# Moving two layer norms and three transposes one step later, splitting the last output block, and sharing the copies of one row between two engines

## The chip, the cores and the metric

The kernel runs on one core of a Trainium2 chip. The metric is the device time of one execution in microseconds (us). Every kernel was executed several times; the numbers below are medians with the range. Runs in the fast state (granted TensorE clock 0.998 to 0.999 of full speed) may be compared with each other.

## The reference, cut to what matters

A sequence of 2048 rows of 640 features goes through two pairs of layers. Layer A is a Fourier filter, layer B an attention over segments of 32 tokens with 32 heads. Both are applied to the layer norm of the row and added to it.

```python
def _layernorm(x, axis=-1, eps=1e-05):
    m = jnp.mean(x, axis=axis, keepdims=True)
    v = jnp.var(x, axis=axis, keepdims=True)
    return (x - m) / jnp.sqrt(v + eps)
...
    x = A_x
    x = x + _A_ref(_layernorm(x, axis=-1), A_w_r, A_w_i)
    x = x + _B_ref(_layernorm(x, axis=-1), B_mem0, B_Wq, B_Wk, B_Wv, B_Wo, B_seg_len)
    x = x + _A_ref(_layernorm(x, axis=-1), A_w_r, A_w_i)
    x = x + _B_ref(_layernorm(x, axis=-1), B_mem0, B_Wq, B_Wk, B_Wv, B_Wo, B_seg_len)
    return x
```

In the kernel the 2048 rows lie as 16 tiles of 128 partitions; a "row" below is such a tile of 128x640.

## The kernel before

Three places matter. The first is the *token stage*, which ends layer A: the inverse transform (tiles `psg`, `psy` in PSUM), the residual add, the statistics and the layer norm of each row, and the transposes of the normed rows that layer B starts from (`pstr`). It runs twice, at 73 and at 835 us. Its loop fixes the order of work on each engine by hand:

```python
LEAD, LAG, EARLY, LAST = 0, 7, 10, 10
ADDED, SQUARED = (0, 1, 2, 3, 4, 6), (1, 3, 6) + (15,)   # rows added by VectorE; rows with statistics by ScalarE
...                                                      # (cut: definitions of the steps)
for i in range(16 + 1):
    ...
    last = i >= LAST
    early = i < EARLY
    ...
    if not early and i % 2 == 1:
        norm((i - 5) // 2)           # norm q: rows 2q and 2q+1, VectorE, needs the inverse deviation of q
    if not last:
        ready(False)                 # statistics on VectorE of the row added a step ago
    if i < 16:
        spectrum_d(i)                # PE: psg i, ScalarE copies it out
    ready(True)                      # statistics on ScalarE, with two small operations of GpSimd
    ...
    for s0 in range(16):
        if turn(s0) == i:
            tokens(s0)               # PE: psy; VectorE or ScalarE adds it to the row
    if early and i >= 5 and i % 2 == 1:
        norm((i - 5) // 2)
    ...
    if i >= 4 and i % 2 == 0:
        inverse((i - 4) // 2, nc.gpsimd)   # six small GpSimd operations, 2.2 us in the trace (80.38 to 82.55)
    ...
    if i >= 8 and i % 4 < 3:         # transposes of a group of four rows, in three parts of 2, 2 and 1 chunks
        n = i % 4
        by_dve_jobs = n != 1 and i < 16
        jobs = handoff.rows_out(handoff.rows_in(pp, xna, i // 4 - 2, 2 * n), by_dve_jobs)
        ...
```

So norm 0 stands in step 5, norm 1 in step 7, norm 2 in step 9, and the first three transposes in steps 8, 9, 10. The tiles `psg` and `psy` share three buffers; the transposes have two.

The second place, called the *seam* below, is the end of the first attention layer, with the first transform of the next layer A row by row (`stage1_tile`), and the verdict of a check inside the kernel, which is read from PSUM (`pc`):

```python
def stage1_tile(self, pp, tag, xn_row, s0):
    nc = self.tc.nc
    for c0, c1 in ((0, 3), (3, 5)):
        ps = pp.tile([128, 512], FP32, name="ps1", tag=tag)
        for ch in range(c0, c1):
            nc.tensor.matmul(ps[:, (ch - c0) * 128:(ch - c0 + 1) * 128], lhsT=xn_row[:, ch * 128:(ch + 1) * 128], rhs=self.T[:, s0, :], start=True, stop=True)
        nc.scalar.copy(out=self.YT[:, c0:c1, :, s0, :], in_=ps[:, 0:(c1 - c0) * 128].rearrange("p (c g k) -> p c g k", c=c1 - c0, k=8))
...
def result(self, flag_col, ranges=False):          # the check's verdict
    nc = self.tc.nc
    vmax = self.tmp("vmax", 1, 1)
    nc.vector.tensor_reduce(out=vmax[:], in_=self.pe[:, 0:self.NC], axis=AX.X, op=ALU.max)      # reads PSUM (pc)
    ...
    nc.vector.tensor_single_scalar(out=ok[:], in_=self.pe[:, self.NC:self.NC + 2], scalar=127.5, op=ALU.is_ge)   # and again
```

After them the spectrum stage opens a new PSUM pool and its first matmuls write the tile `ab`.

The third place is the end of the kernel, the output projection of the last rows:

```python
def run(self, x, lhs_of, psx, first, n_first, pa, xns, check, acc, flag_col):
    ...
    for t in range(16):
        lhs = lhs_of(t)
        for k in (2 * t, 2 * t + 1):
            ps = first[k] if k < len(first) else psx()
            ...
            self.accumulate(ps, k, lhs, n_first if k < len(first) else 0, H)    # 32 matmuls of 320 columns
            c0 = k % 2 * 320
            nc.vector.tensor_tensor(out=x[:, t, c0:c0 + 320], in0=ps[:, 0:320], in1=x[:, t, c0:c0 + 320], op=ALU.add)
        if nxt is None:
            nc.sync.dma_start(out=self.xd[:, t, :], in_=x[:, t, :])
        ...
```

Of the kernel before, what the change touches and what calls it, by code (L numbers as in the profile page):

```python
# [13 lines left out]
ALU = mybir.AluOpType  # L14
# [184 lines left out]
class LayerA:  # L199
# [211 lines left out]
# [3 lines that stand above are left out]
            ps = pp.tile([128, 512], FP32, name="ps1", tag=tag)  # L414
            for ch in range(c0, c1):
                nc.tensor.matmul(ps[:, (ch - c0) * 128:(ch - c0 + 1) * 128], lhsT=xn_row[:, ch * 128:(ch + 1) * 128], rhs=self.T[:, s0, :], start=True, stop=True)
            nc.scalar.copy(out=self.YT[:, c0:c1, :, s0, :], in_=ps[:, 0:(c1 - c0) * 128].rearrange("p (c g k) -> p c g k", c=c1 - c0, k=8))

    def spectrum(self, late_loads=(), handoff=None):
        tc, g, YT, Fd, K = self.tc, self.g, self.YT, self.Fd, self.K  # L420
# [171 lines left out]
    def tokens(self, x_dst, xn_dst, handoff=None):  # L592
        tc, g, UT, Gd, Ti, x = self.tc, self.g, self.UT, self.Gd, self.Ti, self.x
        nc = tc.nc
# [13 lines left out]
            nc.scalar.copy(out=Gs[s0 % 3], in_=psg[:, :, 0:NF])  # L608

        LEAD, LAG, EARLY, LAST = 0, 7, 10, 10  # L610
        ADDED, SQUARED = (0, 1, 2, 3, 4, 6), (1, 3, 6) + (15,)
        nm = wk.tile([128, 16], FP32, name="lnnm", tag="lnnm")

        def tokens(s0):
# [58 lines left out]
        def norm(q):  # L673
            xno = xna[:, 2 * q:2 * q + 2, :]
            for t in range(2):
                _ln_scale(nc, mv[q][:, t:t + 1, :], rs[q][:, t:t + 1], x[:, 2 * q + t:2 * q + t + 1, :], xno[:, t:t + 1, :], 1)
                flush()
            nc.sync.dma_start(out=xnd[:, 2 * q:2 * q + 2, :], in_=xno)

        with tc.manual_schedule(engines={nc.tensor.engine, nc.scalar.engine, nc.vector.engine}):  # L680
            moved, late, by_dve_jobs = [], [], False
            turn = lambda s0: s0 + (2 if LEAD <= s0 < LAG else 1)
            for i in range(16 + 1):
                held = moved if by_dve_jobs else []
                for f in moved if not held else moved[:1]:
                    f()
                held, moved = held[1:], []
                if late:
                    late.pop(0)()
                last = i >= LAST  # L690
                early = i < EARLY
                done = [s0 for s0 in range(16) if turn(s0) == i - 1]
                ready = lambda act: [stats(s0) for s0 in done if (s0 in SQUARED) == act and s0 < 15]
                if last:
                    ready(False)
                if not early and i % 2 == 1:
                    norm((i - 5) // 2)
                if not last:
                    ready(False)
                if i < 16:  # L700
                    spectrum_d(i)
                ready(True)
                for f in held:
                    f()
                    flush()
                for s0 in range(16):
                    if turn(s0) == i:
                        tokens(s0)
                if early and i >= 5 and i % 2 == 1:
                    norm((i - 5) // 2)  # L710
                for f in late:
                    f()
                late = []
                if i >= 4 and i % 2 == 0:
                    inverse((i - 4) // 2, nc.gpsimd)
                if handoff is None:
                    continue
                if i < 10:
                    handoff.wv_piece(i)
                if i == 5:  # L720
                    handoff.memory(pp)
                if i == 16:
                    for s0 in range(10):
                        handoff.add_u(pp, xna[:, s0, :], s0)
                if i >= 8 and i % 4 < 3:
                    n = i % 4
                    by_dve_jobs = n != 1 and i < 16
                    jobs = handoff.rows_out(handoff.rows_in(pp, xna, i // 4 - 2, 2 * n), by_dve_jobs)
                    if n == 1:
                        late = jobs  # L730
                    else:
                        moved = jobs
            flush()
            act_stats(15)
            norm(6)
            inverse(7, nc.vector)
            if handoff is not None:
                for s0 in range(10, 14):
                    handoff.add_u(pp, xna[:, s0, :], s0)
                handoff.do(moved)  # L740
                second = handoff.rows_in(pp, xna, 2, 2)
            norm(7)
            if handoff is not None:
                for s0 in (14, 15):
                    handoff.add_u(pp, xna[:, s0, :], s0)
                handoff.finish(pp)
                handoff.do(handoff.rows_out(second, False))
                pairs = [handoff.rows_in(pp, xna, 3, 2 * n, ps=handoff.big(pp)) for n in range(2)]
                ones = [handoff.rows_in(pp, xna, 2, 4)]
                vb = [handoff.guess1(pp, 0)]  # L750
                ones.append(handoff.rows_in(pp, xna, 3, 4))
                handoff.do(handoff.rows_out(pairs[0], True))
                handoff.do(handoff.rows_out(pairs[1], False))
                vb.append(handoff.guess1(pp, 1))
                handoff.do(handoff.rows_out(ones[0], True))
                handoff.guess1_out(0, vb[0], nc.scalar.copy)
                vb.append(handoff.guess1(pp, 2))
                handoff.guess1_out(1, vb[1], nc.scalar.copy)
                handoff.do(handoff.rows_out(ones[1], True))
                vb.append(handoff.guess1(pp, 3))  # L760
                handoff.guess1_out(2, vb[2], nc.scalar.copy)
                vb.append(handoff.guess1(pp, 4))
                handoff.guess1_out(3, vb[3], nc.vector.tensor_copy)
                handoff.guess1_out(4, vb[4], nc.scalar.copy)
# [773 lines left out]
class _FastOut:  # L1538
# [2 lines left out]
        self.tc, self.g, self.nxt = tc, g, nxt  # L1541
        self.xd = r16(env["x_dst"]) if env["x_dst"] is not None else None

    def accumulate(self, ps, k, lhs, h0, h1):
        c0 = k % 2 * 320
        for h in range(h0, h1):
            self.tc.nc.tensor.matmul(ps[:, 0:320], lhsT=lhs(h, k // 2), rhs=self.g["Wo_sb"][:, h, c0:c0 + 320], start=(h == 0), stop=(h == H - 1))  # L1547

    def run(self, x, lhs_of, psx, first, n_first, pa, xns, check, acc, flag_col):
        nc, nxt = self.tc.nc, self.nxt  # L1550
        early = {t: c for c, t in enumerate((3, 5) if nxt is not None else (3, 5, 7, 9, 11))}
# [3 lines that stand above are left out]
                ps = first[k] if k < len(first) else psx()  # L1555
                if nxt is None and k == 31:
                    self.tc.mark_branch_hint_location("general")
                self.accumulate(ps, k, lhs, n_first if k < len(first) else 0, H)
                c0 = k % 2 * 320
                nc.vector.tensor_tensor(out=x[:, t, c0:c0 + 320], in0=ps[:, 0:320], in1=x[:, t, c0:c0 + 320], op=ALU.add)  # L1560
            if nxt is None:
                nc.sync.dma_start(out=self.xd[:, t, :], in_=x[:, t, :])
            else:
                if t:
                    nxt.stage1_tile(pa, "pss", xns[(t - 1) % 3], t - 1)
                st, mv = _ln_tiles(nc, self.g["ln"])
                _ln_stats(nc, st, mv, x[:, t, :], 0)
                _ln_apply(nc, self.g["ln"], mv, x[:, t:t + 1, :], xns[t % 3].unsqueeze(1), 1, self.g, on_dve=True)
            if t == 2:
                check.prepare(acc)  # L1570
            if t == 4:
                check.begin(acc)
            if t == 6 and nxt is not None:
                nxt.tables(gate=xns[5 % 3][0:1, 0:1])
            if t in early:
                check.block(early[t])
            if t - 1 in early:
                check.vote(early[t - 1])
            if nxt is None and t == 12:
                check.result(flag_col, True)  # L1580
        if nxt is not None:
            for c in range(len(early), 5):
                check.block(c)
            nxt.stage1_tile(pa, "pss", xns[15 % 3], 15)
            for c in range(len(early), 5):
                check.vote(c)
            check.result(flag_col, True)
# [290 lines left out]
```

## Time and profile before

| | us |
|---|---|
| time, median of 3 runs (range) | 1554.5 (1554.37 to 1554.54) |
| profiled span | 1552.9 |
| first token stage, first `psg` to PE's restart on `psu` | 73.22 to 106.72 |
| last `ps` of the first transform to first `ab` | 786.54 to 787.71 |
| end of the last add to the end of the span | 1545.67 to 1552.9 |

The prediction shows the lines of the page and the timelines on which its reading rests. One thing that it does not show is the middle of the token stage in the chain of waits. That view walks back from the last instruction; its columns are start, length, and who did what, with the line of the program. Kernel before:

```profile
80.38 0.24 POOL lnrs L124
80.70 0.74 POOL lnnb L125
...
86.04 0.20 POOL lnrs L129
86.27 0.45 DVE A1tok_S L134
...
91.29 0.20 POOL lnrs L129
91.52 0.80 DVE A1tok_S L134 x2
```

From 80.4 to 86.3, and again up to 91.5, the chain goes through GpSimd (POOL): two inverse deviations in a row, and each time VectorE (DVE) stands at a norm (L134) until GpSimd's last small operation (L129) is through. An inverse took GpSimd 2.2 us (80.38 to 82.55), or 2.7 us with two operations that go with a ScalarE square among its six (88.76 to 91.49); L125 took 0.71 to 0.73 us of that, the others about 0.2. GpSimd is busy for 16% of the span only, and yet it holds the stage here: VectorE started none of its later work while it stood at these norms (1.08 us before the one at 86.27, 0.42 before the one at 91.52).

### The profile page before, as it was taken

Reading aid. Unit: us, or ns where it says so; the run is one execution under the profiler, and the core shown is the slowest. Engines: PE = TensorE matmul, PEld = TensorE weight load, DVE = VectorE, ACT = ScalarE, POOL = GpSimd, SP = SyncE. Lnnn points to the kernel's source line nnn. Section 1 sums busy time; section 2 is a strip of 40 time slices with the busy share of each in tenths; the row PEclk is TensorE's granted clock in tenths of the full one; section 3 lists DMA queues with packets and bytes.
Section 4 is the critical chain, followed back from the end, with each engine's and each line's share of the span. In section 5 each row is a group of like instructions: output and inputs, shape, how many; then the busy total and the mean of one; then the engine's idle time right before and its main releaser. Section 6 shows DMA issues by size and latency. Waiting matters only on the chain.

```text
span 1552.9 us, 36725 instructions
## 1 busy us (share of the span) xinstructions
PE 1535.5 (99%) x14554; PEld 1081.3 (70%) x14555; DVE 816.6 (53%) x2418; ACT 764.9 (49%) x2229; POOL 246.0 (16%) x337
## 2 busy tenths in 40 slices
PE   9999999999999999999999999999999999999997
PEld 7776666666666666777777776666666666667775
DVE  7873555555556545632368545654556545553111
ACT  5574655556555565511126655556555565562000
POOL 2530111112111121100035201112111121110000
PEclk9999999999999999999999999999999999999999
DMA  4780343344533444645114523443434434337241
GB/s 173 230 299 27 111 170 122 137 140 135 178 123 136 136 136 149 201 117 162 51 54 159 178 83 125 136 150 121 172 124 140 148 125 166 124 107 228 79 127 53
DMA packets 168839, 214.90 MB, mean 138 GB/s; under 512 B 8144, under 2 KB 134360, under 8 KB 168656
## 3 DMA queue, kind: packets, MB, share of 16 engines
q1 hardware_dynamic: 168080, 210.15, 40.9%
q8 instruction: 116, 1.90, 0.5%
q0 software_dynamic: 576, 2.30, 0.4%
q14 instruction: 67, 0.55, 0.1%
HBM read 167.32 MB, written 45.10 MB: 137 GB/s over the span
## 4 chain that ended last, share of the span: by engine, by line
PE 92%; DVE 4%; POOL 1%; ACT 1%; issue 1%; DMA 0%; ACTq 0%; DVEq 0%; POOLq 0%
PE psv L1267 19%; PE psk L1201 19%; PE psx L1547 18%; PE psq L1201 18%; PE pso L1351 4%; PE pss L1277 4%; PE ab L449 2%; PE psl L1304 1%; PE psq L1225 1%; PE X L480 1%; PE psu L541 1%; DVE lnst L650 1%; PE psm L977 1%; PE psg L1708 1%; PE psvb L1640 1%
## 5 line engine op out<-in xcount | busy, mean ns | idle before, releaser
L1201 PEld LDWEIGHTS <-bB_S 128*128 128x128 bf16 x3180 | 261.5, 97 | 181.3 <-issue 1.1
L1260 DVE CAST bB_S<-psk 128x495 bf16<-128x495 f32 (+3 forms) x320 | 191.6, 599 | 281.3 <-PE psk L1201 276.9
L1547 PE MATMUL psx<-Wo_sb,bB_S 128*128 128x320 bf16 x2048 | 288.7, 299 | 0.1
L1280 ACT ACTIVATE bB_S<-pss 128x269 bf16<-128x269 f32 (+5 forms) x576 | 208.7, 387 | 138.3 <-PE pss L1277 137.9
L1547 PEld LDWEIGHTS <-bB_S 128*128 128x128 bf16 x2048 | 196.8, 98 | 73.9 <-DVE bB_S L1365 0.7
L1320 POOL TENSOR_TENSOR bB_S<-bB_S,bB_S 128x535 f32<-128x535 f32 x90 | 111.7, 1254 | 795.2 <-DVE bB_S L1312 762.2
L1245 ACT ACTIVATE bB_S<-psq 128x96 bf16<-128x96 f32 x300 | 152.1, 507 | 172.6 <-PE psq L1201 172.6
L1365 DVE TENSOR_TENSOR bB_S<-pso,bB_S 128x480 bf16<-128x480 f32 (+1 forms) x320 | 193.0, 603 | 55.8 <-PE pso L1351 47.2
L1281 DVE TENSOR_TENSOR bB_S<-bB_S,maskf 128x269 bf16<-128x269 bf16 (+5 forms) x576 | 159.5, 290 | 114.3 <-ACT bB_S L1280 114.3
L1269 ACT CAST bB_S<-psv 128x512 bf16<-128x512 f32 (+1 forms) x288 | 162.4, 564 | 81.0 <-PE psv L1267 81.0
L1267 PE MATMUL psv<-bB_S,B1hT_S 128*128 128x256 bf16 x1360 | 168.8, 272 | 0.0
L1267 PE MATMUL psv<-bB_S,B2hT_S 128*128 128x256 bf16 x1360 | 168.8, 272 | 0.0
L1201 PE MATMUL psk<-B1hT_S,bB_S 128*128 128x495 bf16 (+3 forms) x800 | 164.2, 343 | 0.0
L1201 PE MATMUL psk<-B2hT_S,bB_S 128*128 128x495 bf16 (+3 forms) x800 | 164.2, 343 | 0.0
L1201 PE MATMUL psq<-B1hT_S,bB_S 128*128 128x495 bf16 (+5 forms) x780 | 156.0, 336 | 0.5 <-DVE bB_S L1646 0.5
L1201 PE MATMUL psq<-B2hT_S,bB_S 128*128 128x495 bf16 (+5 forms) x780 | 156.0, 336 | 0.5 <-DVE bB_S L1646 0.5
L1267 PEld LDWEIGHTS <-B1hT_S 128*128 128x128 bf16 x1360 | 129.8, 98 | 24.3
L1267 PEld LDWEIGHTS <-B2hT_S 128*128 128x128 bf16 x1360 | 129.8, 98 | 24.3
L1277 PE MATMUL pss<-bB_S 128*128 128x132 bf16 (+8 forms) x1152 | 137.5, 219 | 0.0
L1277 PEld LDWEIGHTS <-bB_S 128*128 128x128 bf16 x1152 | 95.4, 97 | 55.1
L1351 PE MATMUL pso<-bB_S,bB_S 128*128 128x132 bf16 (+8 forms) x1152 | 118.6, 219 | 0.2
L1351 PEld LDWEIGHTS <-bB_S 128*128 128x128 bf16 x1152 | 89.7, 98 | 32.3 <-DVE oTmf L1366 1.9
(299 smaller groups left out, 1438.5 us busy)
## 6 DMA issues: line engine op xcount, KB each, us to landing
bB_S<-Rd SPq DMA_DIRECT2D x124, 535.0 KB
oTx_d<-bB_S SPq DMA_DIRECT2D x60, 512.0 KB
bB_S<-oTx_d SPq DMA_DIRECT2D x46, 512.0 KB
bB_S<-in_B_Wq_dram SPq DMA_DIRECT2D x32, 320.0 KB
bB_S<-in_B_Wk_dram SPq DMA_DIRECT2D x32, 320.0 KB
bB_S<-in_B_Wv_dram SPq DMA_DIRECT2D x32, 320.0 KB
Wo_sb<-in_B_Wo_dram SPq DMA_DIRECT2D x4, 1280.0 KB
B1wv_S<-in_B_Wv_dram SPq DMA_DIRECT2D x10, 512.0 KB
```

Of the source, the lines that this page charges most:

```text
L1201: nc.tensor.matmul(ps, lhsT=w[:, ch, hh * 128:(hh + 1) * 128], rhs=src[:, ch, lo:hi], start=(ch == 0), stop=(ch == 4))
L1245: nc.scalar.mul(out=qv[:, :, 0:SEG], in_=x_view(ps, o, n)[:, :, 1:SW], mul=scale)
L1260: nc.vector.tensor_copy(out=KTs[h % 2][:, lo:hi], in_=ps[:, 0:hi - lo])
L1267: nc.tensor.matmul(ps[:, i * 256:(i + 1) * 256], lhsT=hT[:, ch, st.hcol((t + i) * 128):st.hcol((t + i) * 128) + 128], rhs=w["Wv"][:, ch, : ...
L1269: nc.scalar.copy(out=V[:, t:t + n, :].rearrange("p a b -> p (a b)"), in_=ps[:, 0:n * 256])
L1277: nc.tensor.matmul(ps[:, off - o0:off - o0 + hi - lo], lhsT=KT[:, t * 128:(t + 1) * 128], rhs=QT[:, lo:hi], start=True, stop=True)
L1280: nc.scalar.activation(out=E[:, 0:n], in_=ps[:, 0:n], func=ACTF.Exp)
L1281: nc.vector.tensor_tensor(out=P[:, o0:o0 + n], in0=E[:, 0:n], in1=bs.mask[:, o0:o0 + n], op=ALU.mult)
L1320: nc.gpsimd.tensor_tensor(out=acc, in0=acc, in1=part, op=ALU.add)
L1351: nc.tensor.matmul(pso[:, lo - q0:hi - q0], lhsT=V[:, t, (h % 2) * 128:(h % 2 + 1) * 128], rhs=P[:, off:off + hi - lo], start=(i == 0), st ...
L1365: nc.vector.tensor_tensor(out=oT.rearrange("p (r s j) -> p r s j", r=16, j=2)[:, :, s0:s0 + ns, :], in0=byclass(po), in1=rx, op=ALU.mult)
L1547: self.tc.nc.tensor.matmul(ps[:, 0:320], lhsT=lhs(h, k // 2), rhs=self.g["Wo_sb"][:, h, c0:c0 + 320], start=(h == 0), stop=(h == H - 1))
```

## The change

Its intent is to let the engines find their inputs ready. In the token stage, norms 0 and 1 stand a step later, behind that step's residual add, the first three transposes a step later as well; row 5 is added by VectorE instead of by two identity matmuls and a ScalarE copy, and row 4's statistics go from VectorE to ScalarE. At the seam, VectorE empties the second half of the first transform's last row. At the end, the last 320 columns come in two pieces of 192 and 128, each with its own add and store. The diff, with unchanged context cut:

```diff
@@ stage1_tile
-            nc.scalar.copy(out=self.YT[:, c0:c1, :, s0, :], in_=ps[:, 0:(c1 - c0) * 128].rearrange(...))
+            (nc.vector.tensor_copy if s0 == 15 and c0 else nc.scalar.copy)(out=self.YT[:, c0:c1, :, s0, :], in_=ps[:, 0:(c1 - c0) * 128].rearrange(...))
@@ tokens
-        ADDED, SQUARED = (0, 1, 2, 3, 4, 6), (1, 3, 6) + (15,)
+        ADDED, SQUARED = tuple(range(7)), (1, 3, 4, 6) + (15,)
...
+                due = {6: 0, 8: 1}.get(i, (i - 5) // 2 if i >= 9 and i % 2 else None)
...
-                if not early and i % 2 == 1:
-                    norm((i - 5) // 2)
+                if not early and due is not None:
+                    norm(due)
...
-                if early and i >= 5 and i % 2 == 1:
-                    norm((i - 5) // 2)
+                if early and due is not None:
+                    norm(due)
...
-                if i >= 8 and i % 4 < 3:
-                    n = i % 4
+                if 9 <= i < 12 or i >= 12 and i % 4 < 3:
+                    n = i % 4 - (i < 12)
@@ class _FastOut
-    def accumulate(self, ps, k, lhs, h0, h1):
+    def accumulate(self, ps, k, lhs, h0, h1, lo=0, hi=320):
...
-            self.tc.nc.tensor.matmul(ps[:, 0:320], ..., rhs=self.g["Wo_sb"][:, h, c0:c0 + 320], ...)
+            self.tc.nc.tensor.matmul(ps[:, 0:hi - lo], ..., rhs=self.g["Wo_sb"][:, h, c0 + lo:c0 + hi], ...)
...
                 if nxt is None and k == 31:
                     self.tc.mark_branch_hint_location("general")
+                    for lo, hi in ((0, 192), (192, 320)):
+                        ps = ps if lo == 0 else psx()
+                        self.accumulate(ps, k, lhs, 0, H, lo, hi)
+                        nc.vector.tensor_tensor(out=x[:, t, 320 + lo:320 + hi], in0=ps[:, 0:hi - lo], in1=x[:, t, 320 + lo:320 + hi], op=ALU.add)
+                        nc.sync.dma_start(out=self.xd[:, t, 0 if lo == 0 else 320 + lo:320 + hi], in_=x[:, t, 0 if lo == 0 else 320 + lo:320 + hi])
+                    continue
...
             if nxt is None:
-                nc.sync.dma_start(out=self.xd[:, t, :], in_=x[:, t, :])
+                if t < 15:
+                    nc.sync.dma_start(out=self.xd[:, t, :], in_=x[:, t, :])
```

More of the change, by code (lines that the diff above doesn't have):

```diff
@@ L416, in stage1_tile @@
                 nc.tensor.matmul(ps[:, (ch - c0) * 128:(ch - c0 + 1) * 128], lhsT=xn_row[:, ch * 128:(ch + 1) * 128], rhs=self.T[:, s0, :], start=True, stop=True)
-            nc.scalar.copy(out=self.YT[:, c0:c1, :, s0, :], in_=ps[:, 0:(c1 - c0) * 128].rearrange("p (c g k) -> p c g k", c=c1 - c0, k=8))
+            (nc.vector.tensor_copy if s0 == 15 and c0 else nc.scalar.copy)(out=self.YT[:, c0:c1, :, s0, :], in_=ps[:, 0:(c1 - c0) * 128].rearrange("p (c g k) -> p c g k", c=c1 - c0, k=8))
     def spectrum(self, late_loads=(), handoff=None):
@@ L1542, in __init__ @@
         self.xd = r16(env["x_dst"]) if env["x_dst"] is not None else None
-    def accumulate(self, ps, k, lhs, h0, h1):
+    def accumulate(self, ps, k, lhs, h0, h1, lo=0, hi=320):
         c0 = k % 2 * 320
         for h in range(h0, h1):
-            self.tc.nc.tensor.matmul(ps[:, 0:320], lhsT=lhs(h, k // 2), rhs=self.g["Wo_sb"][:, h, c0:c0 + 320], start=(h == 0), stop=(h == H - 1))
+            self.tc.nc.tensor.matmul(ps[:, 0:hi - lo], lhsT=lhs(h, k // 2), rhs=self.g["Wo_sb"][:, h, c0 + lo:c0 + hi], start=(h == 0), stop=(h == H - 1))
     def run(self, x, lhs_of, psx, first, n_first, pa, xns, check, acc, flag_col):
```

## The prediction

> **What bounds the kernel now.** I read the page first, then the chain that ended last, then the timelines of three stretches that the diff touches.
>
> ```profile
> PE 1535.5 (99%) x14554; PEld 1081.3 (70%) x14555; DVE 816.6 (53%) x2418; ACT 764.9 (49%) x2229; POOL 246.0 (16%) x337
> ```
> ```profile
> PE 92%; DVE 4%; POOL 1%; ACT 1%; issue 1%; DMA 0%; ACTq 0%; DVEq 0%; POOLq 0%
> ```
>
> TensorE (PE) owns 92% of the chain; all else is 8% of 1553 us. The diff leaves the long attention stages alone, so it can only win fractions of a microsecond at a few seams: the two token stages (73 to 107 us, and 835 to 869 us, row for row the same), the seam at 787 us between the first attention layer and the second transform, and the end. First the token stage, VectorE (DVE) alone, then all engines, then the chain:
>
> ```profile
> 82.58 0.80 DVE L134 TENSOR_SCALAR A1tok_S<-A1x_S,lnmv,lnrs 128x640 bf16<-128x640 bf16 x2 [0.69 <-POOL lnrs L129]
> 83.45 0.82 DVE L630 TENSOR_TENSOR A1x_S<-psy,A1x_S 128x640 bf16<-128x640 f32 x1
> 86.27 0.45 DVE L134 TENSOR_SCALAR A1tok_S<-A1x_S,lnmv,lnrs 128x640 bf16<-128x640 bf16 x1 [1.08 <-POOL lnrs L129]
> 91.52 0.80 DVE L134 TENSOR_SCALAR A1tok_S<-A1x_S,lnmv,lnrs 128x640 bf16<-128x640 bf16 x2 [0.42 <-POOL lnrs L129]
> ```
> ```profile
> 84.32 0.99 PE L607 MATMUL psg<-A1gt_S,A1UT_S 128*128 128x321 bf16 x6 [0.35 <-DVE A1x_S L630]
> ...
> 87.20 0.45 PE L1661 MATMUL pstr<-ident,A1tok_S 128*128 128x128 bf16 x5 [0.20 <-DVE A1tok_S L134]
> ...
> 88.72 0.43 PE L622 MATMUL psy<-A1x_S,ident 128*128 128x320 bf16 x2 [0.24 <-DVE A1x_S L633]
> ```
> ```profile
> 102.48 0.13 DVE lnmv L658
> 102.61 0.08 issue
> 102.69 0.31 POOL lnrs L124
> ...
> 106.22 0.46 DVE A1tok_S L134
> 106.67 0.05 issue
> 106.72 0.32 PE psu L1618 x5
> ```
>
> DVE, in program order, stands at norms 0, 1 and 2 (L134) until GpSimd (POOL) has the inverse deviation; behind it wait the PSUM buffers and transposes that PE needs. From 86.27 the chain runs through DVE with hardly a gap up to the last inverse (102.69) and PE's restart at 106.72. So the stage ends when DVE does, with PE hardly less loaded. Now the seam and the end:
>
> ```profile
> 786.95 0.72 ACT A2YT_S L417 x2
> 787.67 0.04 issue
> 787.71 2.92 PE ab L449 x20
> ```
> ```profile
> 1545.18 0.49 DVE L1560 TENSOR_TENSOR bB2x_S<-psx,bB2x_S 128x320 bf16<-128x320 f32 x1 [3.85 <-PE psx L1547]
> 1545.70 0.33 SPq L1562 DMA_DIRECT2D out_dram<-bB2x_S  x1
> ```
> ```profile
> L1834 SPq EVENT_SEMAPHORE  x9: 17/17/17, 1548.9 to 1551.2; - x9
> ...
> L1834 SPq COMPARE_BRANCH  x1: 50/50/50, 1546.1 to 1546.1; - x1
> ```
>
> At 787 us PE waits for two ScalarE (ACT) copies in a row. At the end SyncE issues the last store, branches at 1546.1, executes its first wait past the branch only at 1548.9 and its last at 1551.2.
>
> [...]the POOL L124 took 0.43 us beginning at 91.57, inside DVE's L134, and 0.23 us at 80.38, outside one. I allow 0.2 us for that below.[...] Here 16 transposes of 128 columns took 0.89 us in the chain, 56 ns each[...]. [...] The DMA view agrees that all its packets are over by 1547.5.[...]
>
> **Part 1, the token stage.** Four edits: norms 0 and 1 go one step later, behind that step's residual add; the first three transpose groups go from steps 8, 9, 10 to 9, 10, 11; row 5's residual is added by DVE, so two identity matmuls leave PE (2 x 0.137 = 0.27 us) and a 0.69 us copy leaves ACT; row 4's statistics go from DVE (0.89 + 0.20 busy) to an ACT square (0.83 + 0.19). The order comparison shows just this, and that DVE is in step again at row 11's statistics (97.16 before).
>
> I lay DVE's new order end to end with issue intervals of the old trace (L134 pair 0.71, add 0.85, add with accumulator 0.73, statistics 0.79, transposed copy 0.57 to 0.63), starting at aggregate 2 at 81.68. Add 4 begins at 82.37, as soon as PE has psy 4; norm 0 at 83.1 (its inverse is ready at 82.55); add 5 83.8; statistics 5 84.7; add 6 85.5; norm 1 at 86.4. So norm 1's wait (1.08) all but goes and add 4 comes 1.08 earlier, add 6 2.4 earlier. PE's waits go with them: psg 8 no longer waits (0.5 us of gap at 83.8 to 84.3 by issue intervals), the transposes no longer wait for norm 1 (0.5), psy 8 no longer for add 6 (0.4). What is new: statistics 7 ends near 88.0, but POOL begins inverse 2 only after add 6 (86.3) and needs about 2.7 us (88.76 to 91.49 before), so norm 2 waits until 89.1 to 89.4, a new 1.2 us. The first transpose copies now stand behind norm 2, so the third transpose group, needing the buffer of the first, waits some 0.6 us at 91.8. Continuing: copies 89.9 and 91.3, statistics 9 92.3, norm 3 93.1, statistics 10 94.4, statistics 11 at 96.0 to 96.2 against 97.16. PE comes to step 13 at 94.7 to 94.9 against 95.84. Both are about 1.05 us ahead, and the order behind is unchanged: 1.05 us per stage, of 1.40 + 0.27 = 1.67 that PE's side could give. Two stages: 2.1 us.
>
> **Part 2, the seam.** DVE copies the last 256 columns (0.42 us in the like L523 and L269 rows) as soon as PE has them, about 786.98, so until 787.44; ACT's first copy (from 786.91, 0.48) ends at 787.39. PE starts at about 787.48 for 787.71: 0.23 us. DVE is idle there (its idle before 787.23 is 0.90).
>
> **Part 3, the end.** [...]The last add shrinks from 0.49 to about 0.31 (0.36 for the 128-column L1365 form; 1.03 ns a column between 640 and 320 columns): -0.18. SyncE branches that much sooner: net -0.1. The smaller last store gains nothing itself[...].
>
> Sum: 2.1 + 0.23 + 0.1 = 2.4; 1554.5 - 2.4 = 1552.1 us, 0.16% faster.
>
> **The rivals.** (a) PE is the stage's real limit and norm 2's new wait costs nothing: gain 1.4 to 1.67 a stage, 1551.0 or so. For it: PE's gaps are what the chain restarts on; against: DVE has no slack from 92 to 104. (b) The waits are only moved: norm 2 waits as long as norms 0 and 1 did, [...]because the inserted square (1 us on ACT) holds back psg 8's copy and so psg 9. Then 0.3 to 0.5 a stage, 1553.4. For it: POOL's chain of six small operations is unchanged and ACT is 79 to 86% busy from 83 to 103 us; against: DVE's own work shrinks only slightly, but its order is better matched to arrivals. (c) The last store's landing gates the end[...].[...] (d) Slower by some tenths, if the transposes' delay makes ACT's copies meet at the stage's end: nothing in the order shows it.
>
> **Range and chances.** The token term runs from 0.4 to 1.6 a stage, the other two from 0.1 to 0.6 together: 1551.0 to 1553.5 should hold it 8 times in 10. The old runs differ by 0.17 us. Two per cent is 31 us, more than all waits of PE together, so within 2% is near certain.
>
> **What would show it.** Right: statistics 11 begins about 1 us nearer to the stage's first psy; idle before norm 1 under 0.3, before norm 2 about 1.2; an L1661-type wait of about 0.6 at the third transpose group; ab starts about 0.5 us after the last ps instead of 0.7; the gap from the last add to the end stays 7.2 us. Wrong: norm 2's wait above 2 us, PE's psg 9 waiting for an ACT copy, or a final gap that shrinks with the store.

The sum came to 2.4 us: 2.1 for the two token stages, 0.23 for the seam and 0.1 for the end. Cut from the text above is what no trace or run of this case shows. In the sum that is one term, the loss on the narrower matmuls, which left 0.1 of the add's 0.18 at the end; the trace's own figure for it stands with the result below. Outside the sum it is an explanation of the long L124, an estimate of when the last store lands ("all its packets" are those of that store) and with it the size of rival (c), and the author's reading of the 2.8 us behind the branch: the DMA view has packets on queues that it calls instruction at 1547.0 to 1548.0, inside these 2.8 us, but no view shows what SyncE waits for.

## The result, and the profile after

The changed kernel took 1552.55 us (1552.53 to 1552.77, 5 runs), the kernel before in the same rounds 1554.5 (1554.35 to 1554.54, 5 runs). The ratio is 0.9988, 95% interval 0.9974 to 1.0003. Here and below, a ratio is the mean time of one kernel's fast runs over that of the other's of the same rounds, so it is not quite the ratio of the medians quoted.

Where the profiled spans differ (1552.9 and 1550.9), stretch by stretch:

| stretch | before | after | difference | predicted |
|---|---|---|---|---|
| start to first `psg` | 73.22 | 73.13 | -0.09 | 0 |
| first token stage: chain's first `psg` to restart on `psu` | 33.50 | 32.46 | -1.04 | -1.05 |
| seam: last `ps` to first `ab` | 1.17 | 1.24 | +0.07 | -0.23 |
| second token stage | 33.48 | 32.43 | -1.05 | -1.05 |
| second restart on `psu` to end of last add | 677.01 | 677.05 | +0.04 | -0.1 |
| last add to end of span | 7.23 | 7.33 | +0.10 | 0 |

These sum to -1.97 of the -2.0 in the spans; what lies between the stretches moved by -0.03. The table has a grain: over all fourteen traces PE's first `psg` lies between 72.77 and 73.32 and the last row of the table between 6.91 and 7.63, without relation to what was edited, so times of whole runs cannot settle differences below some 0.5 us; short stretches inside can.

**The token stage.** VectorE's timeline, after (start, length, engine, line, operation, output and inputs, shapes; in square brackets the idle time before it and who ended it):

```profile
82.27 0.82 DVE L633 SCALAR_TENSOR_TENSOR A1x_S<-psy,A1x_S 128x640 bf16<-128x640 f32 x1 [0.35 <-PE psy L626]
83.02 0.80 DVE L134 TENSOR_SCALAR A1tok_S<-A1x_S,lnmv,lnrs 128x640 bf16<-128x640 bf16 x2
...
86.27 0.80 DVE L134 TENSOR_SCALAR A1tok_S<-A1x_S,lnmv,lnrs 128x640 bf16<-128x640 bf16 x2
...
89.08 0.45 DVE L134 TENSOR_SCALAR A1tok_S<-A1x_S,lnmv,lnrs 128x640 bf16<-128x640 bf16 x1 [1.22 <-POOL lnrs L129]
...
96.02 0.86 DVE L650 BATCH_NORM_STATS2 lnst<-A1x_S 128x6 f32<-128x320 bf16 x2
```

Norms 0 and 1 (83.02 and 86.27) have no bracket any more: their inverses are ready. Norm 2 has one of 1.22 us. The statistics of row 11 start at 96.02. PE's timeline after has one wait left between 80 and 97 us, where before had the three that the prediction shows:

```profile
92.35 0.38 PE L1669 MATMUL pstr<-ident,A1tok_S 128*128 128x128 bf16 x4 [0.58 <-DVE B1hT_S L1688]
```

The chain of waits, after:

```profile
85.74 0.15 PE psy L626
85.91 0.70 ACT A1x_S L636
86.61 0.23 POOL lnrs L124
...
88.84 0.21 POOL lnrs L129
89.08 0.45 DVE A1tok_S L134
...
105.08 0.46 DVE A1tok_S L134
105.59 0.32 PE psu L1626 x5
```

Up to 85.9 the chain now runs through PE. One inverse on GpSimd (86.61 to 89.05) is left in it before the stage becomes VectorE's; the last inverse stands in both kernels' chains (from 102.69 before, from 101.56 after).

**The seam.** The timeline of all engines, before:

```profile
786.54 0.44 PE L416 MATMUL ps<-bB_S,bB_S 128*128 128x128 bf16 x5
...
787.23 0.22 DVE L996 TENSOR_REDUCE bB_S<-pc 1x1 f32<-1x70 f32 x1 [0.90 <-PE pc L991]
787.38 0.14 DVE L1001 TENSOR_SCALAR bB_S<-pc 1x2 f32<-1x2 f32 x1
```

and after:

```profile
785.39 0.44 PE L416 MATMUL ps<-bB_S,bB_S 128*128 128x128 bf16 x5
...
785.87 0.42 DVE L417 CAST A2YT_S<-ps 128x256 bf16<-128x256 f32 x1 [0.69 <-PE ps L416]
786.21 0.21 DVE L997 TENSOR_REDUCE bB_S<-pc 1x1 f32<-1x70 f32 x1
786.35 0.14 DVE L1002 TENSOR_SCALAR bB_S<-pc 1x2 f32<-1x2 f32 x1
...
786.63 0.99 PE L449 MATMUL ab<-A2tab_S,A2YT_S 128*128 128x321 bf16 x6 [0.59 <-DVE bB_S L1002]
```

The copy on VectorE takes the 0.42 us that was predicted. But `ab` is now released by L1002, VectorE's second read of the verdict `pc`: `ab` belongs to the pool that is opened after the one with `pc`, and PE stood 0.59 us before its first matmul until that read was over. In the kernel before that read ended at 787.38 + 0.14 = 787.52, while ScalarE's copies ended at 787.67, so this second wait ended 0.15 us before the first and no view names it. The new copy stands ahead of the reads in VectorE's order and puts them from 0.69 us behind `ps` (787.23) to 0.82 us (786.21).

**The end.** VectorE and SyncE in the timeline, after:

```profile
1541.49 0.36 DVE L1562 TENSOR_TENSOR bB2x_S<-psx,bB2x_S 128x192 bf16<-128x192 f32 x1 [2.15 <-PE psx L1548]
1541.88 2.05 SPq L1563 DMA_DIRECT2D out_dram<-bB2x_S  x2
1543.28 0.29 DVE L1562 TENSOR_TENSOR bB2x_S<-psx,bB2x_S 128x128 bf16<-128x128 f32 x1 [1.43 <-PE psx L1548]
```

The adds are 0.36 and 0.29 us. The add before them starts at 1540.84 in the kernel before and at 1538.85 after:

```profile
1540.84 0.49 DVE L1560 TENSOR_TENSOR bB2x_S<-psx,bB2x_S 128x320 bf16<-128x320 f32 x1 [3.85 <-PE psx L1547]
```

```profile
1538.85 0.49 DVE L1567 TENSOR_TENSOR bB2x_S<-psx,bB2x_S 128x320 bf16<-128x320 f32 x1 [3.85 <-PE psx L1548]
```

From there to the end of the last add it is 4.83 us before and 4.72 after. Between the starts of the two adds, time of the matmuls, it is 4.34 us before (1540.84 to 1545.18) and 4.43 after (1538.85 to 1543.28): the narrower matmuls cost 0.09, and the last add gives 0.20 (0.49 to 0.29). The 32 matmuls of 128 columns lie between the starts of the two short adds, 1.79 us or 56 ns each. And SyncE around its branch (number of instructions, then shortest/median/longest in ns, then first and last start):

```profile
L1842 SPq EVENT_SEMAPHORE  x9: 17/17/17, 1546.7 to 1549.2; - x9
...
L1842 SPq COMPARE_BRANCH  x1: 45/45/45, 1544.0 to 1544.0; - x1
```

From the branch to the first wait behind it are 2.7 us, as 2.8 before; both have simply come 2.1 to 2.2 us earlier. What fills this time was not shown.

### The profile page after: what moved, and what is told of

It is laid out like the page before. It is cut to its first block, busy times and chain, and to the rows that moved or that the text cites. A ratio compares the mean times of both kernels' runs of the same rounds, so it can differ in the third digit from the quotient of the medians.

```text
span 1550.9 us, 36788 instructions
## 1 busy us (share of the span) xinstructions
PE 1534.2 (99%) x14582; PEld 1082.4 (70%) x14583; DVE 816.0 (53%) x2418; ACT 765.9 (49%) x2230; POOL 245.9 (16%) x341
## 4 chain that ended last, share of the span: by engine, by line
PE 94%; DVE 3%; ACT 1%; POOL 1%; issue 1%; DMA 0%; DVEq 0%; ACTq 0%; POOLq 0%
PE psv L1268 19%; PE psk L1202 19%; PE psx L1548 18%; PE psq L1202 18%; PE pso L1352 4%; PE pss L1278 4%; PE ab L449 2%; PE psl L1305 1%; PE psq L1226 1%; PE psg L607 1%; PE X L480 1%; PE psu L541 1%; PE psm L978 1%; PE psg L1716 1%; DVE lnst L650 1%
## 5 line engine op out<-in xcount | busy, mean ns | idle before, releaser
L1548 PE MATMUL psx<-Wo_sb,bB_S 128*128 128x320 bf16 (+2 forms) x2080 | 288.7, 297 | 0.1
```

What stands on the lines that cost most here:

```text
L1548: self.tc.nc.tensor.matmul(ps[:, 0:hi - lo], lhsT=lhs(h, k // 2), rhs=self.g["Wo_sb"][:, h, c0 + lo:c0 + hi], start=(h == 0), stop=(h == H ...
```

## The experiments

Twelve kernels were run, on three chips. All gave correct results. The size of a token stage is given below as PE's first `psg` to the last matmul group on `psu` (mean of both stages): 33.65 us in the kernel before, 32.61 in the changed one. (The table above takes the chain's first `psg`, 0.16 later.) The kernel before took 1553.91 us (1553.78 to 1554.42, 9 runs) beside runs 1 to 4, 1554.41 (1554.19 to 1555.63, 7 runs) beside runs 5 to 8, and 1553.98 (1553.82 to 1554.42, 9 runs) beside runs 9 to 12.

### 1. token_only: the token stage's edits alone

```diff
 # the kernel before, with the edits of tokens(): ADDED, SQUARED, due, norm(due), transposes
```

> The kernel before plus the token-stage edits alone. Theory 1 (ledger of the two traces: 1.04 and 1.05 us per token stage, nothing else of size): 1552.4 us, the restart of PE at the 50 psu matmuls 33.5 us after the stage's first psg in the kernel before, 32.45 here, in both stages. Rival (seam and end give the rest of the gain as the prediction had it, 0.33 us): 1552.9.

1552.18 us (1552.0 to 1552.26, 5 runs), ratio 0.9988. Stages 32.60 and 32.59, seam 1.17 as in the kernel before. As far as the grain lets one see, the token edits alone give the whole of the change's gain (1.73 us in the medians here, 1.95 for the change).

### 2. no_token: the seam and the end alone

```diff
 # the changed kernel, with the edits of tokens() undone
```

> The changed kernel without its token-stage edits: only the two-engine emptying and the split last block are left. Theory 1: nothing worth measuring, 1554.5 within 0.15; ab starts 1.24 us after the last ps against 1.17 before, and the end is about 0.1 us nearer. Rival (the prediction's terms, 0.23 + 0.1): 1554.2.

1554.51 us (1554.1 to 1554.77, 5 runs), ratio 1.0002. Stages 33.66 and 33.64, seam 1.24. The other two parts together save nothing that can be seen in the time: this median lies 0.6 us above that of the kernel before, about the size of the grain. Whole runs could not settle the 0.33 us that the prediction gave the two parts; the stretches do, with +0.07 at the seam and about -0.1 at the end.

### 3. norm2_later: norm 2 a step later too

```diff
-                due = {6: 0, 8: 1}.get(i, (i - 5) // 2 if i >= 9 and i % 2 else None)
+                due = {6: 0, 8: 1, 10: 2}.get(i, (i - 5) // 2 if i >= 11 and i % 2 else None)
```

> The changed kernel with norm 2 also a step later, behind the first transposed copy and statistics 8, so that VectorE has work while GpSimd ends inverse 2. Theory 1 (VectorE's 1.22 us wait before norm 2 and the 0.58 us that PE then waits for the transpose buffer are real cost, VectorE and PE together set the stage's end): 0.7 to 0.8 us less per stage, 1551.0 us; idle before norm 2 gone, no PE wait at the third transpose group. Rival (PE or ScalarE alone set the end, or the wait only moves on to another norm): 1552.3 to 1552.6.

1550.92 us (1550.86 to 1551.04, 5 runs), ratio 0.998, interval 0.9966 to 0.9994. Stages 31.89 and 31.88, 0.73 below the changed kernel. VectorE's timeline:

```profile
88.13 0.74 DVE L1684 COPY B1hT_S<-pstr 128x480 bf16<-128x480 bf16 x1 [0.19 <-PE pstr L1669]
...
89.84 0.43 DVE L134 TENSOR_SCALAR A1tok_S<-A1x_S,lnmv,lnrs 128x640 bf16<-128x640 bf16 x1
```

VectorE copies the first transposes while GpSimd works, and norm 2 comes 0.76 us later by the clock but without a wait; PE has no wait at the third transposes either. So the new wait of the changed kernel was real cost, and it was the order's, not GpSimd's: GpSimd's last operation of that inverse starts at 88.84 after and at 88.92 here.

### 4. pc_by_act: ScalarE copies the verdict, VectorE reads the copy

```diff
-        vmax = self.tmp("vmax", 1, 1)
-        nc.vector.tensor_reduce(out=vmax[:], in_=self.pe[:, 0:self.NC], axis=AX.X, op=ALU.max)
+        vmax, pe = self.tmp("vmax", 1, 1), self.pe
+        if ranges:
+            pe = self.tmp("pcs", 1, self.NC + 2)
+            nc.scalar.copy(out=pe, in_=self.pe[:, 0:self.NC + 2])
+        nc.vector.tensor_reduce(out=vmax[:], in_=pe[:, 0:self.NC], axis=AX.X, op=ALU.max)
...                                  # and the second read from pe as well; all on top of the changed kernel
```

> The changed kernel, but the 72 values of the check's PSUM row pc are brought to SBUF by one ScalarE copy, and VectorE works on that. Theory 2 (at the seam PE's first ab matmul waits until VectorE has read pc[...], and the new copy on VectorE stands in front of these reads): ab starts about 1.0 us after the last ps instead of 1.24, 1552.3 us. Rival (the copy on VectorE itself is what PE waits for): ab starts as late as in the changed kernel, 1552.55.

1552.03 us (1551.72 to 1552.92, 5 runs), ratio 0.9988; stages as in the changed kernel, seam 1.05 instead of 1.24. The timeline of all engines (`ps` began at 785.30):

```profile
786.04 0.20 ACT L999 COPY bB_S<-pc 1x72 f32<-1x72 f32 x1
...
786.35 0.85 PE L449 MATMUL ab<-A2tab_S,A2YT_S 128*128 128x321 bf16 x5 [0.40 <-ACT bB_S L999]
```

With VectorE's reads of PSUM out of the way, `ab` starts 0.19 us nearer to `ps`, and what releases it is again a read of `pc`, now ScalarE's (over at 786.24, 0.11 us before `ab`). That shows the cause: in the changed kernel `ab` waits for the last reader of `pc`, and not for the copy on VectorE. Little more can be had here: that copy ends at 786.20 (785.78 + 0.42), only 0.04 before ScalarE's read of `pc`. The time of the whole run is too coarse to show 0.19 us.

### 5. norms_only: the kernel before, norms 0 and 1 later

```diff
+                due = {6: 0, 8: 1}.get(i, (i - 5) // 2 if i >= 9 and i % 2 else None)
 # and norm(due) in both places, as in the change; rows and transposes as before
```

> The kernel before with only norms 0 and 1 a step later. Theory 1, laid out by hand from the durations of the trace before: psg 8 and psy 8 wait no more, add 6 at about 85.5 instead of 87.85, inverse 2 and with it norm 2 about 1.5 us earlier (its copies in front of it fill VectorE), but the first transposes, still in step 8, wait about 1 us for norm 1; PE about 0.5 us ahead, then 0.3 more from waits that VectorE no longer causes: 0.5 to 0.9 us per stage, 1.0 to 1.8 in all. Rival (the parts only work together): under 0.2 per stage.

1553.5 us (1553.28 to 1553.66, 4 runs), ratio 0.9993. Stages 33.18 and 33.17: -0.48, just short of the range expected. Norm 1 no longer waits, but PE now stands at the first transposes for it (PE's timeline):

```profile
87.18 0.81 PE L1662 MATMUL pstr<-ident,A1tok_S 128*128 128x128 bf16 x6 [0.84 <-DVE A1tok_S L134]
```

### 6. rows_only: the kernel before, rows 4 and 5 as in the change

```diff
-        ADDED, SQUARED = (0, 1, 2, 3, 4, 6), (1, 3, 6) + (15,)
+        ADDED, SQUARED = tuple(range(7)), (1, 3, 4, 6) + (15,)
```

> The kernel before with only row 5's residual on VectorE and row 4's statistics on ScalarE. Theory 1: norm 1 still stands in VectorE's order waiting for GpSimd until about 86.3, and all that follows it (statistics 5, add 6) is as before: 0 to 0.1 us per stage although PE has two matmuls (0.27 us) less. Rival (PE's own work is the bound): 0.27 per stage, 0.55 us in all.

1554.93 us (1554.85 to 1555.48, 4 runs), ratio 1.0002. Stages 33.85 and 33.86: +0.21, where nothing or a small gain had been expected. VectorE's timeline tells why:

```profile
86.60 0.80 DVE L134 TENSOR_SCALAR A1tok_S<-A1x_S,lnmv,lnrs 128x640 bf16<-128x640 bf16 x2 [1.56 <-POOL lnrs L129]
```

VectorE has less to do ahead of norm 1 and so waits longer for it (1.56 against 1.08), and the inverse itself comes 0.33 later (L129 at 86.37 for 86.04), since GpSimd now has row 4's small operations among those of inverse 1 (L663, 0.24 us from 86.06).

### 7. transposes_only: the kernel before, transposes later

```diff
-                if i >= 8 and i % 4 < 3:
-                    n = i % 4
+                if 9 <= i < 12 or i >= 12 and i % 4 < 3:
+                    n = i % 4 - (i < 12)
```

> The kernel before with only the first three transpose groups a step later. Theory 1: the transposes of step 8 no longer fit into the time that PE waits for add 6 anyway, and the transposed copies come to stand behind norm 2, which waits until 91.5: slower by 0.5 to 1.3 us per stage, 1 to 2.6 us in all. Rival (less waiting of the transposes for norm 1 is a gain of its own): faster by up to 0.5 per stage.

1557.17 us (1556.84 to 1557.54, 4 runs), ratio 1.0017. Stages 35.01 and 34.98: +1.35, just over the range expected. VectorE's timeline:

```profile
91.54 0.45 DVE L134 TENSOR_SCALAR A1tok_S<-A1x_S,lnmv,lnrs 128x640 bf16<-128x640 bf16 x1 [2.00 <-POOL lnrs L129]
...
92.33 0.74 DVE L1676 COPY B1hT_S<-pstr 128x480 bf16<-128x480 bf16 x1
```

Norm 2 starts when it did before (91.52), but in the kernel before VectorE filled the time with two copies of transposes (0.69 and 0.76 us) and waited only 0.42. Now they come behind the norm.

### 8. one_store: the changed kernel with a single last store

```diff
-                        nc.sync.dma_start(out=self.xd[:, t, 0 if lo == 0 else 320 + lo:320 + hi], in_=...)
+                    nc.sync.dma_start(out=self.xd[:, t, :], in_=x[:, t, :])    # after both adds
```

> The changed kernel, last block still in two pieces, but one store of all 640 columns after the second add. Theory 3 (SyncE's own branch[...] set the end; the store lands before): as the changed kernel, within 0.1 us; the time from the last add to the end the same 7.1 to 7.4 us. Rival (the store's landing sets the end)[...].

1552.47 us (1552.3 to 1552.99, 4 runs), ratio 0.9986, like the changed kernel's. From the last add's end to the span's end it is 6.97 us, just under the 7.1 to 7.4 expected and within the scatter named above. SyncE around the branch:

```profile
L1842 SPq EVENT_SEMAPHORE  x9: 17/17/17, 1547.2 to 1549.5; - x9
...
L1842 SPq COMPARE_BRANCH  x1: 50/50/50, 1544.6 to 1544.6; - x1
```

Again 2.6 us pass behind the branch, with five times the bytes in the last store (160 KB against 32 KB). The store's last packets start before 1546.2, 1 us ahead of that wait at 1547.2; in the kernel before they are over by 1547.5, against 1548.9. The traces don't show the landing itself, and the final gap scatters by 0.7 us (6.91 to 7.63), but nothing here points to the store as what sets the end.

### 9. best: runs 3 and 4 together

```diff
 # the changed kernel with the edits of norm2_later and of pc_by_act
```

> The changed kernel with norm 2 a step later and ScalarE copying the verdict row so that VectorE reads it from SBUF. Theory (the two gains lie in different stretches and add up): token stages as in the run with norm 2 later, 0.73 us each below the changed kernel (about 31.7 us from the first psg to the restart on psu), seam from last ps to ab 1.05 us instead of 1.24; in all 1.6 us below the changed kernel and 3.5 us below the kernel before, so near 1550.7 when the kernel before takes 1554.4. Rival (the seam's gain is noise, because that run's median was 0.5 under the changed kernel with a spread of 1.2 us): same time as norm 2 later alone, about 1551.0, and a seam of 1.2.

1550.61 us (1550.5 to 1551.08, 5 runs), ratio 0.9978, interval 0.9965 to 0.9992: 3.37 us under the kernel before of the same rounds. Stages 31.88 and 31.87, seam 1.05: each stretch has the size it had in its own run, so the two gains do not disturb each other. Against norm2_later (2.99 us under its own kernel before) the whole run gains 0.4, of which the seam explains 0.19 and the rest is within the grain. This is the fastest version.

### 10. transposes_back: the changed kernel, transposes as before

```diff
-                if 9 <= i < 12 or i >= 12 and i % 4 < 3:
-                    n = i % 4 - (i < 12)
+                if i >= 8 and i % 4 < 3:
+                    n = i % 4
```

> The changed kernel with the first three transpose groups back at steps 8, 9, 10 (norms and rows stay changed). The stage is measured from the first psg to the last psu: before 33.66, changed 32.62, each part alone 33.18 (norms), 33.85 (rows), 35.01 (transposes). Theory A (the transposes have to move because norm 1 now comes later; PE would otherwise stand at the first transpose group until norm 1 is through): 33.0 to 33.4, a PE wait of 0.4 to 1.0 us before the first transposes, no long wait at norm 2. Theory B (the transposes' move only costs, as alone, and norms with rows carry the gain): 32.0 to 32.6, as fast as the changed kernel or faster.

1552.82 us (1552.75 to 1552.9, 4 runs), ratio 0.9992. Stages 32.93 and 32.90: just under theory A's range and above theory B's. PE's timeline:

```profile
86.59 0.81 PE L1669 MATMUL pstr<-ident,A1tok_S 128*128 128x128 bf16 x6 [0.79 <-DVE A1tok_S L134]
```

The wait that theory A named is there, and VectorE has none before norm 2. The transposes' move, worth +1.35 alone, is worth -0.31 here.

### 11. norms_back: the changed kernel, norms as before

```diff
-                due = {6: 0, 8: 1}.get(i, (i - 5) // 2 if i >= 9 and i % 2 else None)
 # and the two conditions of the kernel before
```

> The changed kernel with norms 0 and 1 back at steps 5 and 7 (rows and transposes stay changed). Theory A (the norms' move is what frees VectorE's order; without it norm 1 stands 1.5 us as in the run with rows alone and the late transposes add norm 2's wait): raw stage 34.0 to 35.3, slower than before. Theory B (parts add up from the single runs, 33.66+0.19+1.35): 35.2. The wait before norm 1 should be 1.3 to 1.7 us and before norm 2 1.5 to 2.2 us.

1557.52 us (1557.21 to 1557.79, 4 runs), ratio 1.0022. Stages 35.17 and 34.93. Both theories allowed this size, so it does not tell them apart; the two waits of VectorE are those that were named. PE also stands 1.16 us before the `psg` at 87.65 for a ScalarE copy (L608), the kind of wait that the prediction's rival (b) feared for the changed kernel. VectorE's timeline:

```profile
86.38 0.80 DVE L134 TENSOR_SCALAR A1tok_S<-A1x_S,lnmv,lnrs 128x640 bf16<-128x640 bf16 x2 [1.56 <-POOL lnrs L129]
...
91.53 0.45 DVE L134 TENSOR_SCALAR A1tok_S<-A1x_S,lnmv,lnrs 128x640 bf16<-128x640 bf16 x1 [1.96 <-POOL lnrs L129]
```

### 12. rows_back: the changed kernel, rows 4 and 5 as before

```diff
-        ADDED, SQUARED = tuple(range(7)), (1, 3, 4, 6) + (15,)
+        ADDED, SQUARED = (0, 1, 2, 3, 4, 6), (1, 3, 6) + (15,)
```

> The changed kernel with rows 4 and 5 back (row 5 added by PE, row 4's statistics on VectorE); norms and transposes stay changed. Theory A (the rows matter only as 0.27 us less PE work and 1.09 us less VectorE work, which shows once VectorE is the bound after 92 us): raw stage 33.0 to 33.5, 0.4 to 0.9 above the changed kernel. Theory B (rows do nothing, as alone): 32.6, as the changed kernel.

1553.67 us (1553.26 to 1553.91, 4 runs), ratio 0.9997. Stages 33.17 and 33.16, in theory A's range, but not by the path that A named (less work once VectorE is the bound, after 92 us): the loss is there before. VectorE's timeline:

```profile
89.71 0.45 DVE L134 TENSOR_SCALAR A1tok_S<-A1x_S,lnmv,lnrs 128x640 bf16<-128x640 bf16 x1 [1.53 <-POOL lnrs L129]
```

Norm 2's inverse is ready 0.63 later than in the changed kernel, because GpSimd starts on it at 87.20 instead of 86.61: in its order it stands behind a small operation on row 6's sum, and VectorE comes to that row's add later, with row 4's statistics to do before; PE's wait at the third transposes is 0.99 instead of 0.58.

### The three token edits together

Runs 1, 5, 6, 7, 10, 11 and 12 and the kernel before are all eight combinations. Stage in us (mean of the two) and its distance from before:

| norms later | rows | transposes later | stage | difference |
|---|---|---|---|---|
| no | no | no | 33.65 | |
| yes | no | no | 33.18 | -0.48 |
| no | yes | no | 33.86 | +0.21 |
| no | no | yes | 35.00 | +1.35 |
| yes | yes | no | 32.92 | -0.73 |
| no | yes | yes | 35.05 | +1.40 |
| yes | no | yes | 33.17 | -0.48 |
| yes | yes | yes | 32.60 | -1.05 |

The three alone sum to +1.08; together they give -1.05. Only the norms' move gains by itself. It brings the add of row 6 forward, and with it GpSimd's inverse 2: that is the inverse for rows 4 and 5, but in GpSimd's order it stands behind a small operation that needs row 6's sum. GpSimd starts on it at 87.29 with the norms' move alone and at 86.61 with all three, instead of 89.06, and only where it comes early does another edit gain. The rows' edit then gains 0.26 (33.18 to 32.92). The transposes' move on top of the norms alone changes nothing (33.18 to 33.17); it gains 0.32 only with the rows as well. Which of the two rows makes the rows' edit pay was not tested, since they were always moved together.

## Why the prediction was right or wrong

**Right: the token stage**, -1.05 each, measured -1.04 and -1.05. Its steps can be followed one by one in the timelines above: add 4 predicted at 82.37, came at 82.27; norm 1 at 86.4, came at 86.27; norm 2's new wait 1.2 until 89.1 to 89.4, came as 1.22 until 89.08; PE's wait at the third transposes about 0.6, came as 0.58; statistics 11 at 96.0 to 96.2, came at 96.02. What made it work was to lay out VectorE's new order with the issue intervals of the old trace and to ask at every norm when GpSimd could have begun. The 0.2 us allowed there, because L124 took 0.43 us inside a norm and 0.23 outside one in the kernel before, was not needed. In the changed kernel GpSimd's L663 at 83.19 took 0.34 us inside a norm (83.02 to 83.82), but its L663 at 86.31 and L124 at 86.61 took 0.22 and 0.23 inside another (86.27 to 87.07); so what lengthens such operations stays open here. Runs 1 and 2 show that the gain is this part's alone.

**One sentence of its reading was too smooth.** "From 86.27 the chain runs through DVE with hardly a gap": the chain leaves VectorE for GpSimd from 88.76 to 91.5. The calculation allowed for it (inverse 2 and its 2.7 us), but the sentence hid where the next gain was: run 3 took it, 0.73 us a stage.

**Right in the block itself, not seen in the time: the end.** From the start of the add before to the end of the last add, the five traces with the old end have 4.83 or 4.84 us, the nine with two pieces 4.71 or 4.72: -0.1, as predicted. Over the longer stretch from the second restart on `psu` this drowns. The five with the old end have 676.99 to 677.02 there, the eight with two pieces and two stores 676.87 to 677.12 (median 676.89), and one_store, whose edit touches only the store, has 677.32. The changed kernel's own trace shows +0.04. The final gap shows no change beyond its scatter.

**Wrong: the seam.** The step that failed is "PE starts at about 787.48 for 787.71: 0.23 us" with its ground, "DVE is idle there". It measured +0.07; by the prediction's own sign, from the end of the last `ps` to `ab`, 0.80 us for the 0.5 expected and the 0.73 before. The duration of the copy was right. What was missed is a second condition on `ab`, the reads of `pc`, which in the kernel before would alone have allowed a gain of 787.67 - 787.52 = 0.15 us at most, and which the new copy pushes back by 0.13. With the 0.14 us that pass between the end of that read and `ab` in the changed kernel, an estimate closes: before, the read would have let `ab` start at 787.66 instead of 787.71, a gain of 0.05, and 0.13 later makes it a loss of 0.08, near the 0.07 measured. The idle time before 787.23 belonged to an instruction that somebody waits for, and ending it later was not free. Run 4 shows it by taking VectorE's reads out. Even then `ab` starts 1.05 behind `ps` and not the 0.94 predicted (787.48 - 786.54).

**The rivals.** (a), PE as the limit with 1.4 to 1.67 a stage, falls: norm 2's wait did cost, and run 3, which removes it, gains 1.77 a stage over the kernel before, so the room that (a) saw was there but behind this wait. (b), the waits are only moved, holds for a part: norm 2's 1.22 and PE's 0.58 are moved waits, yet smaller than those that went. (c), the store's landing, finds nothing for it in run 8: five times the bytes made the final gap no longer (6.97 us for 7.33). (d), slower, did not come; runs 7 and 11 show that it was near, 1.4 us a stage with the norms left where they were.

The sum was 2.4 and the medians moved by 1.95. Of the 0.45 between them, the seam accounts for 0.30; the rest is smaller than the scatter of start and end.

## What to carry to other kernels

VectorE worked in program order here (norm 2's wait went from 1.22 us to none when the norm moved behind ready work), so a wait for a small, slow helper is cheapest when the waiting instruction stands behind other work that is ready: find for each such instruction when its input can be there, and place it just after (0.73 us a stage in run 3). Edits to an order need not add up, so try them together and undo them one by one, as here +1.35 alone became -0.31 in company. And before an idle engine is given work at a seam, look at what its next instruction releases, also where the profile names another releaser that came a tenth of a microsecond later (0.15 us at the seam, which came out at +0.07 for -0.23).
